# Top-k attention and a tanh-shrink FFN on one core: batch 0's key and query rows in 256-byte runs turned by TensorE, weight exponents by one ScalarE operation

## The chip, the core and the metric

The kernel runs on one core of a Trainium2 chip. The metric is the device time of one execution in microseconds (us), lower is better. All inputs and outputs lie in the chip's memory; transfers go through the core's 16 DMA engines. Five engines run their own instruction queues in order and wait for each other on semaphores: TensorE (PE in the profile, with its weight loads as PEld), VectorE (DVE), ScalarE (ACT), GpSimd (POOL) and SyncE (SP), which only issues DMAs here.

## What is computed

The reference does attention with 8 batches, 8 heads, 576 tokens and a head size of 64. Of each row of scores only the 32 largest stay. The result, 4608 rows of 512, goes through a two-layer network with a tanh shrink.

```python
scores = scale * np.matmul(q, k.transpose(0, 1, 3, 2))
kth = np.partition(scores, -top_k, axis=-1)[..., -top_k:-top_k + 1]   # top_k = 32
scores = np.where(scores >= kth, scores, -1e9)
attn = np.exp(scores - np.max(scores, axis=-1, keepdims=True))
attn = attn / (np.sum(attn, axis=-1, keepdims=True) + 1e-09)
x = np.matmul(attn, v)            # then (B, H, S, D) -> (B*S, H*D) = (4608, 512)
h = x @ w_in                      # (512, 2048)
out = (h - np.tanh(h)) @ w_out    # (2048, 512)
```

q, k and v arrive as 32-bit floats. The weights w_in and w_out arrive as 64-bit floats, and the kernel turns them into 32-bit floats itself.

## The kernel before

**Steps.** The attention is cut into steps. A step takes two heads (a head pair `hp`, 0 to 3) of one batch and 128 query rows (`qt`), or the 64 rows that are left over of two pairs. The order is written out by hand (`tc.manual_schedule()`): the main loop in `run` goes over `n` and issues, for each `n`, work of several steps at once: the top-32 search of step n (`search`), the mask of step n-1 (`mask`), the turning of the probabilities of step n-2 (`turn_pe` while batch 0 lasts, `turn_z` after it), the scores of step n+1 (`scores`), the exponentials of step n-1 (`expo`), and pieces of the network (`ffn_h`, `ffn_o`), which `deal` hands out at a rate worked out from the steps alone. The program is therefore the same list per engine whatever the times are; only the waits move.

**What a step asks of each engine.** VectorE does the search: two passes that split the scores into larger and smaller halves (L268, L269), a check (L271), and then four rounds of "eight largest" (L276) with three "replace these eight" (L279). ScalarE copies the scores out of PSUM (L246), makes the mask (L308) and the exponentials (L331). GpSimd makes the thresholds (L295), subtracts the mask (L311, two instructions of 1.4 us back to back) and notes suspicious rows (L315). TensorE makes the scores (L238), turns the probabilities in batch 0 (L425, with ScalarE copying the result out of PSUM in L428), multiplies by v (L453) and does the network (L504, L525).

**Batch 0.** Its first four steps, n = 0 to 3, are the four head pairs with query rows 0 to 127. The keys and queries of all four pairs are loaded ahead of the loop's first steps by `load_rows`, in the order pair 0, weight piece 0, pair 1, weight piece 1, and so on. Pair 0 goes to a load buffer; pairs 1 to 3 go to `early`, slices of `w_in[2]` and `w_in[3]`, whose place is free until those weights are converted. One `load_rows` makes four DMAs. Each has 32 partitions with 18 runs of 32 floats (128 bytes) in each, so that a plain 32 by 32 block transpose on VectorE (`turn_rows`, L223) gives the keys or queries with the head dimension on the partitions. Pair hp is turned during step hp-1, after the first round of the search (`at_round[(n - 1, 0)]`), keys and queries one after the other. `scores` of step hp wait for both. The PSUM pool `zt_ps`, two buffers, serves `turn_pe` and `values`.

**Weights.** `convert` handles a piece of 128 by 512 weights. Two DMAs of 512 KB bring it (L148 as it is, L149 shifted by three bytes). Then:

- VectorE takes the 11 exponent bits (L158), ScalarE clamps and rescales them in two operations (L159, L162), VectorE cuts the mantissa (L164), ScalarE scales it (L167);
- VectorE joins sign and exponent (L170), where L162's result lies in PSUM for the 16 pieces of w_in (`e`) and in SBUF for the 16 pieces of w_out (`f`, in place);
- GpSimd multiplies the two (L173).

Pieces 0 and 1 belong to step 0, pieces 2 and 3 to step 1, three pieces to each of steps 2 to 9, four to step 10. Within a step the parts are spread over the rounds of the search, the first after round 0, behind the turning of keys and queries. A piece's buffer is loaded again when L173 has been issued; seven buffers exist at the start.

Of the kernel before, what the change touches and what calls it, by code (L numbers as in the profile page):

```python
# [8 lines left out]
AF = mybir.ActivationFunctionType  # L9
ALU = mybir.AluOpType  # L10
FP32 = mybir.dt.float32
I32 = mybir.dt.int32
# [7 lines left out]
J = 4  # L20
# [29 lines left out]
def kernel(  # L50
# [9 lines left out]
    nc = tc.nc  # L60
    P = nc.NUM_PARTITIONS
    B, H, S, D = q.shape
    DM, DFF = moe_w_in.shape
    NHP = H // 2
    JP = J * P
    R = S - JP
# [10 lines left out]
    scale = 1.0 / float(D) ** 0.5  # L77
# [5 lines left out]
    def pool(name, bufs, **kw):  # L83
        return ctx.enter_context(tc.tile_pool(name=name, bufs=bufs, **kw))

    consts = pool("consts", 1)
# [12 lines left out]
    zt_ps = pool("zt_ps", 2, space=PS)  # L99
    h_ps = pool("h_ps", 2, space=PS)  # L100

    ident = consts.tile([P, P], FP32, name="ident")
# [3 lines left out]
    w_in = [consts.tile([P, CD, DFF // WJ], FP32, name=f"w_in{j}") for j in range(WJ)]  # L106
# [8 lines left out]
    zx1 = consts.tile([P, 4 * S], FP32, name="zx")[:]  # L115
    et2 = [consts.tile([P, 4 * S], FP32, name="et")[:], later[:, 0 : 4 * S]]
    et_rem = later[:, 4 * S : 6 * S]
    e1151 = consts.tile([P, 1], FP32, name="e1151")
    nc.gpsimd.memset(e1151[:], 1151.0 * 2.0**23)
    e255 = consts.tile([P, 1], FP32, name="e255")  # L120
    nc.gpsimd.memset(e255[:], 255.0 * 2.0**23)

    def flat(x):
        return x.rearrange("p n w -> p (n w)")
# [13 lines left out]
    def convert(piece, slot):  # L138


        j, i = piece // CD, piece % CD
        if j < WJ:
            src, dst = moe_w_in[i * P : (i + 1) * P, j * NW : (j + 1) * NW], w_in[j][:, i, :]
        else:
            r0 = ((j - WJ) * FJ + i) * P
            src, dst = moe_w_out[r0 : r0 + P, :], w_out[j - WJ][:, i, :]
        raw, shifted, _ = slot
        nc.sync.dma_start(flat(raw), src.bitcast(U32))  # L148
        nc.sync.dma_start(  # L149
            flat(shifted).bitcast(U8)[:, 0 : 8 * NW - 4], src.bitcast(U8)[:, 3 : 8 * NW - 1]  # L150
        )
        yield
        hi = raw[:, :, 1]
        f = thpool.tile([P, NW], FP32, tag="th", name="f")
        fu = f[:].bitcast(U32)


        nc.vector.tensor_scalar(fu, hi, 20, 0x7FF, ALU.logical_shift_right, ALU.bitwise_and)  # L158
        nc.scalar.activation(f[:], fu, AF.Relu, bias=e1151[:], scale=-(2.0**23))  # L159

        e = h_ps.tile([P, NW], FP32, tag="h", name="e")[:] if j < WJ else f[:]
        nc.scalar.activation(e.bitcast(I32), f[:], AF.Relu, bias=e255[:], scale=-1.0)  # L162

        nc.vector.tensor_scalar(  # L164
            dst.bitcast(U32), shifted[:, :, 0], 0x0FFFFFFF, None, ALU.bitwise_and
        )
        nc.scalar.activation(dst, dst.bitcast(U32), AF.Copy, bias=1.0, scale=2.0**-28)  # L167
        yield

        nc.vector.scalar_tensor_tensor(  # L170
            out=fu, in0=hi, scalar=0x80000000, in1=e.bitcast(U32), op0=ALU.bitwise_and, op1=ALU.bitwise_or
        )
        nc.gpsimd.tensor_tensor(dst, dst, f[:], ALU.mult)  # L173
        yield
# [3 lines left out]
    raw, kT, qT, vb, vr = {}, {}, {}, {}, {}  # L178
# [5 lines left out]
    def half(t):  # L184
        return slice(t * D, (t + 1) * D)


    early = [flat(w_in[j][:])[:, i * S : (i + 1) * S] for j in (2, 3) for i in range(3)]

    def load_rows(name, b, hp, exact):  # L190

        if b == 0 and hp and not exact:
            x = early[2 * hp - 2 + (name == "q")]
        else:
            x = ldpool.tile([P, S], FP32, tag=f"{name}in", name=f"{name}in")[:]
        raw[name, b, hp] = x
        src = {"k": k, "q": q}[name]
        for a in range(NG):
            h, d = 2 * hp + a // 2, a % 2 * G
            queue = nc.scalar if a and (name, b, hp, exact) == ("q", 0, 0, False) else nc.sync  # L200
            queue.dma_start(  # L201
                x[a * G : (a + 1) * G, :].rearrange("i (n d) -> i n d", d=G),
                src[b, h, :, d : d + G].rearrange("(n i) d -> i n d", i=G),
            )

    def load_v(b, hp):
# [4 lines left out]
        for t in range(2):  # L211
# [4 lines left out]
            o = 0 if t else JP  # L216
            nc.sync.dma_start(y[half(t), t, :], v[b, h, o : o + R, :])

    def turn_rows(name, b, hp):

        d = kqpool.tile([P, S], FP32, tag=f"{name}T", name=f"{name}T")
        {"k": kT, "q": qT}[name][b, hp] = d
        nc.vector.transpose(d[:], raw.pop((name, b, hp)))  # L223

# [183 lines left out]
    def turn_pe(n):  # L410

        g, z = steps[n], st.pop(n)["z"]
        if g.rem:
            et = et_rem
        elif g.i:
            et = ets.pop(n - 1)
        else:
            et = et2[0]
        ets[n] = et
        et = tiles(et, g.nq)[:, :, :, g.i, :].rearrange("p a k j -> p k a j")  # L420
        for k0 in range(0, KC, J):
            kn = min(J, KC - k0)
            zt = zt_ps.tile([P, 512], FP32, tag="zt", name="zt")
            for k in range(kn):
                nc.tensor.transpose(  # L425
                    zt[:, k * P : (k + 1) * P], z[:, (k0 + k) * P : (k0 + k + 1) * P], ident[:]
                )
            nc.scalar.copy(  # L428
                et[:, k0 : k0 + kn],
                zt[:, 0 : kn * P].rearrange("p (k a j) -> p k a j", a=NG, j=G),  # L430
            )
            if k0:
                yield
# [119 lines left out]
    def plan():  # L553
        steps.clear(), done.clear()

        def block(b, qt):
            return [(slice(0, P), out[b * S + qt * P : b * S + (qt + 1) * P, :])]

        rest = None
        for b in range(B):  # L560
            if b % 2 == 0:
                rest = Unit(
                    [[(half(i), out[(b + i) * S + JP : (b + i + 1) * S, :]) for i in range(2)]], "xTr"
                )

            parts = [(0, 1), (2, 3)]
            if b == 0:
                parts[0:1] = [(0,), (1,)]
            for a, qts in enumerate(parts):
                unit = Unit([block(b, qt) for qt in qts], "xT")  # L570
                pe = b == 0
                for hp in range(NHP):
                    for i, qt in enumerate(qts):
                        steps.append(Step(b, hp, qt, unit, 0, i, len(qts), pe))
                    if hp == NHP - 1:
                        done[len(steps) - 1] = unit
                    if hp % 2 and a == (0 if b == B - 1 else len(parts) - 1):
                        steps.append(Step(b, hp - 1, J, rest, b % 2 * R, pe=pe))
                        if hp == NHP - 1 and b % 2:
                            done[len(steps) - 1] = rest  # L580
        for g, after in zip(steps, steps[1:]):
            if after.pe and not after.rem and not g.pe:
                g.lag = 3
# [3 lines left out]

    def run(exact):
        plan()
        NS = len(steps)  # L590
        todo, at_round, turned = {}, {}, {}

# [5 lines left out]
        for i, (b, hp) in enumerate(pairs):  # L598
            n = next(n for n, g in enumerate(steps) if (g.b, g.hp) == (b, hp))
            for x, name in enumerate("kq"):  # L600
                m = max(n - 5 + x, turned.get(name, -4))
                if b == 0 and not exact:
                    m = -4
                at(m, lambda x=(name, b, hp, exact): load_rows(*x))
                if x and i < NHP and not exact:
                    at(-4, lambda: load_piece())
                turn = lambda x=(name, b, hp): turn_rows(*x)
                if 0 < i < NHP:
                    at_round.setdefault((n - 1, 0), []).append(turn)
                    turned[name] = n - 1  # L610
                else:
                    at(n - 3 + x, turn)
                    turned[name] = n - 3 + x
            at(n + 1 if b else n - 1, lambda b=b, hp=hp: load_v(b, hp))
# [41 lines left out]
        def here(i):  # L656
            return 0 <= n + i < NS

# [25 lines left out]
        def rate():  # L684
# [3 lines left out]
            coming = sorted((t, u.n // 8) for u, t in ready.items() if t > n)  # L688
            for t, k in coming + [(NS + LAG, 0)]:
                r = have / max(t - n, 1)  # L690
# [18 lines left out]

        for n in range(-4, NS + LAG):  # L710
            pe = here(-2) and steps[n - 2].pe
            for m in (n - LAG, n - LAG + 1, n - LAG + 2):
                if 0 <= m < NS and steps[m].last and steps[m].lag == n - m:
                    values(m)
            share, usable = rate(), converted[0]
            if pe:
                w = turn_pe(n - 2)
# [74 lines left out]
```

## Time and profile before

| | |
|---|---|
| time, median of 3 (lowest to highest) | 1534.32 us (1533.35 to 1534.38) |
| span of the profiled execution | 1533.0 us |
| busy: TensorE, VectorE, ScalarE, GpSimd | 1432.2, 1349.9, 1021.6, 871.3 us |
| chain that ended last, by engine | TensorE 75%, VectorE 13%, ScalarE 5%, SyncE 2%, DMA 2% |
| VectorE's start of the search (L268) in steps 0 to 11 | 10.31, 22.41, 35.58, 49.07, 61.77, 73.92, 86.19, 99.16, 115.04, 128.80, 146.21, 163.18 us |
| L223, keys and queries of pairs 1 to 3 | 3 x 768 ns and 3 x 736 ns |
| L159 | 32 x 711 ns |
| L162 | 16 x 692 ns into PSUM, 16 x 722 ns into SBUF |
| L428, ScalarE copy out of PSUM | 589 ns for 512 columns, 267 ns for 128 |

Busy times are sums over a whole run and hide that the kernel has stages. Two tools of the profile show them: the span cut into slices with the busy share of each engine, and the timeline, in which every row is one instruction (or several of a kind, xN) with its start, its duration, and in brackets how long its engine sat idle before it and what it waited for. A duration can itself hold a wait that no semaphore shows.

### The profile page before, as it was taken

What the parts mean: (1) busy time and instruction counts of PE and PEld (TensorE: products, weight loads), DVE (VectorE), ACT (ScalarE), POOL (GpSimd) and SP (SyncE); (2) the same over time, 40 slices, a digit from 0 to 9 for tenths busy, and PEclk for the clock granted to TensorE, in tenths of its full rate; (3) what the DMA queues carried; (4) which work ended last, traced back from release to release, by engine and by line L of the source; (5) the groups of instructions that cost most, each with busy time, mean ns of one, the idle gap of its engine ahead of it and who ended that gap; (6) DMA issues with size and microseconds to landing.
All of it is one profiled execution on the core that took longest, in us unless ns stands there. A gap on an engine that the chain in (4) does not pass through costs nothing.

```text
span 1533.0 us, 24064 instructions
## 1 busy us (share of the span) xinstructions
PE 1432.2 (93%) x7302; PEld 901.9 (59%) x7302; DVE 1349.9 (88%) x3884; ACT 1021.6 (67%) x1833; POOL 871.3 (57%) x1371
## 2 busy tenths in 40 slices
PE   2567898999999999999999999999999999999997
PEld 1355566456465675656575665656565665656673
DVE  7998999999999999999999999999999999997100
ACT  4887777667676676767676676767676676767320
POOL 3777676656474564647474574647475574746210
PEclk9887999999999999999999999999999999999999
DMA  9944113556755666556655565556655666543400
GB/s 256 358 169 161 50 24 95 148 142 163 168 140 176 144 151 156 140 157 153 171 136 157 144 157 165 138 144 157 174 140 148 148 155 164 140 140 91 137 8 16
DMA packets 255467, 221.61 MB, mean 145 GB/s; under 512 B 197728, under 2 KB 204896, under 8 KB 248160
## 3 DMA queue, kind: packets, MB, share of 16 engines
q1 hardware_dynamic: 253552, 219.75, 53.4%
q8 instruction: 60, 0.98, 0.3%
q14 instruction: 79, 0.65, 0.2%
q10 hardware_dynamic: 1776, 0.22, 0.1%
HBM read 136.17 MB, written 83.76 MB: 143 GB/s over the span
## 4 chain that ended last, share of the span: by engine, by line
PE 75%; DVE 13%; ACT 5%; SPq 2%; DMA 2%; POOL 1%; issue 1%; DVEq 0%; ACTq 0%; POOLq 0%
PE ops L525 29%; PE hps L504 28%; PE av L453 9%; PE scps L238 8%; DVE m L276 3%; DVE ab L279 3%; DVE zx L388 2%; SPq L201 1%; DVE ab L269 1%; DVE ab L271 1%; DVE ab L268 1%; DMA zx<-in_moe_w_in_dram 1%; PE zt L425 1%; ACT z L308 1%; ACT sc L246 1%
## 5 line engine op out<-in xcount | busy, mean ns | idle before, releaser
L525 PE MATMUL ops<-w_out,g 128*128 128x512 f32 x1152 | 525.6, 603 | 0.0
L311 POOL TENSOR_TENSOR z<-sc,z 128x576 f32<-128x576 f32 x288 | 401.0, 1415 | 209.0 <-ACT z L308 209.0
L504 PE MATMUL hps<-xT,w_in 128*128 128x256 f32 (+1 forms) x2176 | 475.1, 374 | 0.5 <-ACT g L517 0.4
L276 DVE MAX8 m<-ab 128x8 f32<-128x288 f32 (+1 forms) x1152 | 468.4, 450 | 0.0
L504 PEld LDWEIGHTS hps<-xT,w_in 128*128 128x128 f32 x2176 | 391.6, 193 | 82.5 <-issue 32.3
L279 DVE MATCH_REPLACE8 ab<-m,ab 128x288 f32<-128x288 f32 x864 | 377.2, 446 | 0.0
L525 PEld LDWEIGHTS ops<-w_out,g 128*128 128x128 f32 x1152 | 211.3, 191 | 256.8 <-issue 240.6
L518 POOL TENSOR_TENSOR g<-g,th 128x512 f32<-128x512 f32 x144 | 182.8, 1274 | 159.3 <-ACT g L517 154.5
L308 ACT ACTIVATE z<-sc,tb 128x576 f32<-128x576 f32 x288 | 207.6, 769 | 89.7 <-POOL tb L295 78.2
L238 PE MATMUL scps<-kT,qT 64*128 64x288 f32 (+1 forms) x1280 | 188.2, 445 | 42.3 <-DVE qT L223 27.1
L331 ACT ACTIVATE z<-z,nb 128x576 f32<-128x576 f32 x288 | 221.2, 771 | 2.5 <-POOL z L311 2.4
L388 DVE STREAM_TRANSPOSE zx<-z 128x1152 f32<-128x1152 f32 x126 | 172.6, 1370 | 42.8 <-ACT z L357 42.5
L357 ACT ACTIVATE z<-z,rd 128x576 f32<-128x576 f32 x252 | 180.3, 763 | 44.3 <-DVE rd L350 44.3
L238 PEld LDWEIGHTS scps<-kT,qT 64*128 64x128 f32 (+1 forms) x1280 | 102.3, 184 | 130.4 <-issue 42.4
L246 ACT COPY sc<-scps 128x1152 f32<-128x1152 f32 x144 | 159.2, 1105 | 11.3 <-PE scps L238 10.2
L341 POOL TENSOR_SCALAR rd<-den 128x2 f32<-128x2 f32 x144 | 33.5, 233 | 198.6 <-ACT z L331 197.6
L516 ACT ACTIVATE th<-hps 128x512 f32<-128x512 f32 x144 | 84.8, 589 | 89.9 <-PE hps L504 87.5
L268 DVE TENSOR_TENSOR ab<-scps,sc 128x576 f32<-128x576 f32 x144 | 105.7, 734 | 13.9 <-ACT sc L246 6.5
L271 DVE MAX8 ab<-ab 128x8 f32<-128x288 f32 x288 | 116.2, 445 | 0.0
L269 DVE TENSOR_TENSOR ab<-scps,sc 128x576 f32<-128x576 f32 x144 | 107.4, 746 | 0.0
L453 PE MATMUL av<-et,vb 128*64 128x256 f32 (+1 forms) x640 | 77.2, 373 | 30.4 <-ACT et L428 30.4
L535 ACT COPY ot<-ops 128x512 f32<-128x512 f32 x36 | 21.0, 584 | 114.3 <-PE ops L525 114.3
(70 smaller groups left out, 1157.5 us busy)
## 6 DMA issues: line engine op xcount, KB each, us to landing
there<-zx SPq DMA_DIRECT2D x56, 1152.0 KB, 4.2
spare<-there SPq DMA_DIRECT2D x112, 288.0 KB, 5.3
et<-there SPq DMA_DIRECT2D x112, 288.0 KB, 5.1
kin<-in_k_dram SPq DMA_DIRECT2D x116, 72.0 KB, 2.4
vb<-in_v_dram SPq DMA_DIRECT2D x64, 128.0 KB, 5.7
out_dram<-ot SPq DMA_DIRECT2D x32, 256.0 KB, 2.3
qin<-in_q_dram SPq DMA_DIRECT2D x113, 72.0 KB, 3.1
there<-zx SPq DMA_DIRECT2D x14, 576.0 KB, 4.8
```

The lines of the kernel that those rows point to most:

```text
L238: nc.tensor.matmul(ps[rows, t, s, 0:S2], qT[g.b, g.hp + i][half(t), qs], kT[g.b, g.hp + i][half(t), ks], start=True, stop=True,)
L276: nc.vector.max(m[:, t, m8], last[t] if i == rounds - 1 else cur[t])
L279: nc.vector.match_replace(nxt[t], m[:, t, m8], cur[t], NEG)
L308: nc.scalar.activation(zv[:, t, :], scf[:, t, :], AF.Relu, bias=tb[:, t : t + 1], scale=-BIG)
L311: nc.gpsimd.tensor_tensor(zv[:, t, :], scf[:, t, :], zv[:, t, :], ALU.subtract)
L331: nc.scalar.activation(x["zv"][:, t, :], x["zv"][:, t, :], AF.Exp, bias=x["nb"][:, t : t + 1], scale=scale, accum_out=den[:, t : t + 1],)
L357: nc.scalar.activation(x, x, AF.Copy, scale=rds[n][:, g.i, t : t + 1])
L388: nc.vector.transpose(tiles(zx, g.nq)[:, :, :, g.i, :].rearrange("p c k j -> p k c j"), z[:].rearrange("p (k c j) -> p k c j", c=NG, j=G),)
L453: nc.tensor.matmul(av[half(t), 0, cols], vb[g.b, hp][:, t, c, :] if c < J else vr[g.b, hp][:, t, :], es[:, :, (J + 1) * t + c if c < J els ...
L504: nc.tensor.matmul(cur[u][:, s : s + w], w_in[j][:, c, fo : fo + P], u.xT[:, c, 0:w], start=(c == 0), stop=(c == CD - 1),)
L518: nc.gpsimd.tensor_tensor(g, g, th[:], ALU.subtract)
L525: nc.tensor.matmul(cur[u][:], u.g[o // 1024][:, o % 1024 // 512, o % 512 : o % 512 + P], w_out[f // FJ][:, f % FJ, :], start=(f == 0), sto ...
```

## The change

Two edits. The first makes the loads of the keys and queries of batch 0's pairs 1 to 3 in runs of 256 bytes: tokens lie on the partitions, and for each head one DMA brings 512 tokens (128 partitions, 4 runs each) and one brings the last 64. Such rows can't be turned by VectorE's 32 by 32 transpose; TensorE turns them, four 128 by 128 transposes and one of 64 rows for each of keys and queries, and ScalarE copies the two PSUM tiles out. A row is then 640 floats wide, so the `early` slices grow. The second edit makes the exponent of a weight with one ScalarE operation in place of two. Its aim is less work on ScalarE, the first one's is fewer small transfers at the start and less work on VectorE.

```diff
-    e1151 = consts.tile([P, 1], FP32, name="e1151")
-    nc.gpsimd.memset(e1151[:], 1151.0 * 2.0**23)
-    e255 = consts.tile([P, 1], FP32, name="e255")
-    nc.gpsimd.memset(e255[:], 255.0 * 2.0**23)
+    e896 = consts.tile([P, 1], FP32, name="e896")
+    nc.gpsimd.memset(e896[:], -896.0 * 2.0**23)
...
         nc.vector.tensor_scalar(fu, hi, 20, 0x7FF, ALU.logical_shift_right, ALU.bitwise_and)
-        nc.scalar.activation(f[:], fu, AF.Relu, bias=e1151[:], scale=-(2.0**23))
         e = h_ps.tile([P, NW], FP32, tag="h", name="e")[:] if j < WJ else f[:]
-        nc.scalar.activation(e.bitcast(I32), f[:], AF.Relu, bias=e255[:], scale=-1.0)
+        nc.scalar.activation(e.bitcast(I32), fu, AF.Relu, bias=e896[:], scale=2.0**23)
...
-    early = [flat(w_in[j][:])[:, i * S : (i + 1) * S] for j in (2, 3) for i in range(3)]
+    early = [flat(w_in[j][:])[:, 5 * i * P : 5 * (i + 1) * P] for j in (2, 3) for i in range(3)]
...
+        if b == 0 and hp and not exact:
+            xv = x.rearrange("p (c t d) -> p t c d", t=2, d=D)
+            for t in range(2):
+                h = 2 * hp + t
+                nc.sync.dma_start(
+                    xv[:, t, 0:J, :], src[b, h, 0:JP, :].rearrange("(c p) d -> p c d", p=P)
+                )
+                nc.sync.dma_start(xv[0:R, t, J, :], src[b, h, JP:S, :])
+            return
...
-        nc.vector.transpose(d[:], raw.pop((name, b, hp)))
+        x = raw.pop((name, b, hp))
+        if not (b == 0 and hp and turned_pe[0]):
+            nc.vector.transpose(d[:], x)
+            return
+        for c0, c1, w in ((0, J, P), (J, J + 1, R)):
+            zt = zt_ps.tile([P, 512], FP32, tag="zt", name="zt")
+            for c in range(c0, c1):
+                o = (c - c0) * P
+                nc.tensor.transpose(zt[:, o : o + w], x[0:w, c * P : (c + 1) * P], ident[0:w, 0:w])
+            w = (c1 - c0 - 1) * P + w
+            nc.scalar.copy(d[:, c0 * P : c0 * P + w], zt[:, 0:w])
```

More of the change, by code (lines that the diff above doesn't have):

```diff
@@ L217, in load_v @@
             nc.sync.dma_start(y[half(t), t, :], v[b, h, o : o + R, :])
+    turned_pe = [True]
     def turn_rows(name, b, hp):
@@ L589, in run @@
         plan()
+        turned_pe[0] = not exact
         NS = len(steps)
```

## The prediction, made before the changed kernel was built

> **What bounds the kernel now.** I read the slices of the span first, then busy time by stretches, then the waits and the timeline of the start, since the change touches only steps 0 to 10.
>
> ```profile
> PE   2567898999999999999999999999999999999997
> DVE  7998999999999999999999999999999999997100
> ACT  4887777667676676767676676767676676767320
> ```
>
> A slice is 38.3 us. TensorE is not full in the first six slices and full from there to the end; VectorE is nearly full from the second slice.
>
> ```profile
> 0.00:38.00 38.00, 8.84 (x32) 5.23 (x32) 27.40 (x72) 16.55 (x25) 11.68 (x27) 1.00 1.04 256
> 38.00:76.00 38.00, 20.75 (x109) 14.45 (x110) 36.54 (x105) 32.13 (x58) 28.05 (x37) 0.84 0.99 358
> 76.00:115.00 39.00, 25.80 (x192) 21.41 (x190) 35.20 (x99) 33.14 (x60) 28.86 (x37) 0.85 0.48 171
> 115.00:153.00 38.00, 27.70 (x153) 20.40 (x153) 30.71 (x83) 29.88 (x57) 28.58 (x38) 0.73 0.45 162
> 268.00:400.00 132.00, 123.17 (x584) 70.38 (x583) 132.00 (x387) 92.50 (x165) 79.17 (x131) 0.99 0.58 150
> 600.00:800.00 200.00, 200.00 (x976) 126.78 (x974) 193.43 (x557) 140.86 (x254) 120.21 (x192) 1.00 0.58 150
> ```
>
> Columns: stretch, length, busy time of TensorE, its weight loads, VectorE, ScalarE, GpSimd, then clock, DMA share and GB/s. Up to 38 us the DMAs are full (1.04) at only 256 GB/s: small packets. To 76 us VectorE is the fullest engine, 36.54 of 38. From 76 to 153 us no engine is full, so the steps hang on a loop through several. At 268 to 400 us VectorE is busy 132.00 of 132, later TensorE 200.00 of 200. Work after step 10 is unchanged and in the same order, and its limits are those two engines. So **what the start saves moves the end one for one**, and nothing else can.
>
> Who waits for whom on VectorE, first up to 60 us, then 60 to 160 us (total, times, longest):
>
> ```profile
> DVE w_in L164 <- DMA w_out<-in_moe_w_in_dram: 3.5, 3, 1.3
> DVE f L158 <- DMA w_out<-in_moe_w_in_dram: 1.7, 2, 1.3
> DVE f L170 <- ACT f L162: 10.9, 4, 4.6
> ```
>
> In steps 0 and 1 VectorE waits for weight pieces, behind the small packets on the rings; in steps 7 to 10 it waits for the exponent, the operation that the second edit shortens.
>
> **What the Trainium skill says.** Three places. "SBUF — State Buffer", section "Who interferes with whom": VectorE in a two-port mode, or with two SBUF inputs, and a GpSimd instruction exclude each other, and the second to issue blocks until the first is done. The trace agrees:
>
> ```profile
> 25.08 2.76 POOL L311 TENSOR_TENSOR z<-sc,z 128x576 f32<-128x576 f32 x2 [0.41 <-ACT z L308]
> 26.03 0.77 DVE L223 STREAM_TRANSPOSE kT<-w_in 128x576 f32<-128x576 f32 x1
> 26.72 0.73 DVE L223 STREAM_TRANSPOSE qT<-w_in 128x576 f32<-128x576 f32 x1
> 27.39 0.74 DVE L158 TENSOR_SCALAR f<-w_out 128x512 uint32<-128x512 uint32 x1
> ```
>
> L158 takes 0.41 us where GpSimd is quiet; here 0.74, ending at 28.13, 0.29 after L311's end at 27.84. L223 isn't held up. L170 with `f` in SBUF (w_out) takes 0.68 free and 1.35 against L311; with `e` in PSUM it is never held.
>
> "DMA: Bandwidth & Descriptors", section "Why small descriptors are slow (HBM only)": a fixed cost of about 3 cycles per packet, 11 cycles for 256 bytes; by the same rule 7 for 128 bytes, an estimate, so 256 bytes cost 1.57 times as much. The packet records up to 60 us give 15.5 ns per packet of 128 bytes and 18.0 of 256 (1.16 times); over the whole run 13.6 and 21.4 (1.57 times, in agreement).
>
> "TensorE: Matmul & The Clock Gate", section "Part 4: PE-mode transpose": the transpose ends in PSUM and needs a copy; some 275 ns each in a kernel. Row L425 shows eight in 1.97 us at 34.72, 246 ns each, and I use that.
>
> **The change part by part.**
>
> *Loads.* 24 DMAs of 576 packets, 13,824 packets of 128 bytes, become 6,912 of 256. On 16 engines: 13,824 x 15.5 / 16 = 13.4 us become 7.8 us (18.0 ns), 9.2 (21.4 ns) or 10.5 (1.57 x 15.5). Saved: 5.6, 4.2 or 2.9 us. I take 4.2. SyncE's issues number 24 both times; the v loads of the same new shape cost it 0.4 to 0.65 us each, and the present ones about 0.8[...]; nothing is lost there. Piece 1 lies behind two of the six loads (1.4 us earlier), piece 3 behind all.
>
> *Turning.* Off VectorE: in each of steps 0 to 2, 0.77 + 0.73 less overlap, 1.36 us (26.03 to 27.39). On TensorE: 5 transposes per turn, 1.2 us, while it is idle for 29 of the first 38 us. On ScalarE: 0.59 + about 0.22 per turn (L428, from 512 columns and from 128), 1.6 us per step. Behind these copies on ScalarE stand the step's conversions, and the queries' transposes wait for the keys' copies since `zt_ps` has two buffers: about 4 us until both are there. In steps 1 and 2 they follow L308, after which ScalarE idles 2.50 us before L159 now; L159's removal gives back 0.71 per piece. The scores that wait for the turn are needed only at the next L268, 8 us later. **Cost on the path: nothing.**
>
> *Exponent.* 32 x 711 ns, 22.7 us off ScalarE. The one operation that stays is taken at L162's 0.69 and 0.72; nothing shows it with integers on both sides, so 0.6 to 0.75. Its worth depends on what the step hangs on.
>
> *Step 0 and 1.* Step 0: VectorE comes to piece 1 1.36 us sooner but piece 1 only 1.4 to 1.9 sooner: gain 1.4 to 1.9, say 1.6. Step 1: without L223, L158 arrives at 26.03 of the old clock, inside the first of the two L311 (25.08 to 26.45). If it gets the port between the two, it ends at 26.8 in place of 28.13: gain 1.3. Then the DMA waits of piece 3 (0.41 + 0.86) fall away if the piece comes 4.2 us sooner. 1.6 + 1.3 + 1.3 = 4.2; the DMA allows 2.9 to 5.6. **4.0 taken.**
>
> *Step 2.* L158 at 40.55 takes 1.18 us, ending 0.29 after L311 at 41.45. Without L223 it arrives at 39.20, in the first L311, and goes at 40.07: **gain 1.3**, or 0 if the port is not given up.
>
> *Steps 3 to 5.* Here ScalarE looks critical, but the lock decides:
>
> ```profile
> 66.58 2.89 POOL L311 TENSOR_TENSOR z<-sc,z 128x576 f32<-128x576 f32 x2 [1.37 <-ACT z L308]
> 68.53 0.69 DVE L170 SCALAR_TENSOR_TENSOR f<-w_out,e 128x512 uint32<-128x512 uint32 x1
> 69.13 0.61 DVE L158 TENSOR_SCALAR f<-spare 128x512 uint32<-128x512 uint32 x1
> ```
>
> L158 of the third piece waits for L311's end (69.47) and ends 0.28 later. Getting there 0.4 to 0.6 us sooner only lengthens its wait. L311 hangs on L308, that on TensorE's turn (L425, L428), that on GpSimd's L369 behind L173, that on VectorE's L170: a loop of 12.2 us without L159 in it. **Gain 0.**
>
> *Steps 6 to 10.* The same loop, but now the first L170 has two SBUF inputs:
>
> ```profile
> 107.00 2.79 POOL L311 TENSOR_TENSOR z<-sc,z 128x576 f32<-128x576 f32 x2 [2.45 <-ACT z L308]
> 107.47 0.72 ACT L159 ACTIVATE f<-f,e 128x512 f32<-128x512 uint32 x1
> 108.22 0.72 ACT L162 ACTIVATE f<-f,e 128x512 int32<-128x512 f32 x1
> 108.97 1.35 DVE L170 SCALAR_TENSOR_TENSOR f<-spare,f 128x512 uint32<-128x512 uint32 x1 [3.07 <-ACT f L162]
> ```
>
> L170 misses the gap between the two L311 (108.37) and waits for the second (109.79). Without L159 the exponent is there at 108.2, 0.1 to 0.2 before the gap; the same in steps 8, 9, 10. If L170 gets in, it ends 1.35 sooner, of which about 0.8 reaches the next step, since GpSimd's own queue (L311, L315, two L173) then sets the third L170. If not, 0.1. Steps 7 to 10: 3.2 or 0.4. **2.5 taken**, because VectorE did get in between L311 and L315, as at 28.13.
>
> Sum: 4.0 + 1.3 + 0 + 2.5 = 7.8 us. 1534.3 - 7.8 = 1526.5.
>
> **Rivals.**
>
> *The lock is never given up between two L311.* Then removing L223 buys only waiting; the DMA waits go (1.3 + 1.3) and 0.5 elsewhere: 3.1 us, 1531.2. For it: the two L311 start back to back. Against: the L315 case.
>
> *ScalarE is the bound from step 3.* Then every wait for it goes: 10.9 (above) plus 1.2 for L246 and 0.6 for the PSUM exponent, 12.7, plus the 5.3 of steps 0 to 2: 18 us, 1516.3. For it: the chain of waits names L159, L162, L167 and L246 in a row from 76 to 160 us. Against: the lock and the loop, which it doesn't show.
>
> *The turn adds waits.* ScalarE and TensorE need about 4 us for what took VectorE 1.5; if the 2.6 us show up in three steps, 7.8 us stand against the 4.0 saved by the loads: 1538.1, slower. For it: conversions queue behind the copies. Against: the idle 2.50 us before L159.
>
> **How the numbers follow.** Forecast 0.50, lock 0.21, ScalarE 0.20, turn 0.09. The bounds of the forecast itself are 1522 to 1531. Faster by over 0.2% (under 1531.2): 0.50 + half of the lock case 0.10 + 0.20 = 0.80. Within 0.2%: the rest of the lock case and a small turn cost, 0.13. Slower 0.07. Range 1515.5 to 1533: it takes in the ScalarE case and the lock case and leaves out the turn case and the tails.
>
> **What would show it.** L164 of step 0 should wait for a DMA under 1.3 us and those of step 1 not at all; L268 of step 3 should start some 5 us sooner (44 us); steps 3 to 5 should still last 12.2 us each with L158 of the third piece ending 0.3 after L311; steps 7 to 10 should show L170 of the first w_out piece between the two L311. From step 11 on, spacings should be unchanged. The prediction is wrong if steps 4 to 6 become much shorter than 12 us, if L238 waits for L428-like copies into the next L268, or if time gained by 163 us is given back before 400 us.

## The result and the profile after

The changed kernel takes **1527.41 us** (median of 6 runs, 1526.02 to 1529.87) against 1533.62 us of the kernel before on the same chip (6 runs, 1532.89 to 1534.38): ratio 0.9962, 95% interval 0.9949 to 0.9974. The profiled span went from 1533.0 to 1526.4 us.

The diff moves line numbers. After the change L286 starts the search (before: L268), L329 is the mask subtraction on GpSimd (L311), L155, L160 and L166 are VectorE's three parts of a weight piece (L158, L164, L170), L158 is the exponent (L159 and L162), L169 GpSimd's product (L173). L239 and L241 are the new transposes and copies; L233 is what is left of the transpose on VectorE.

The slices of the span, answering to those of before:

```profile
PE   4567898999999999999999999999999999999997
DVE  7998999999999999999999999999999999997100
ACT  4776777767676676767676676767676676767320
```

TensorE's first digit rose from 2 to 4 (the turns), ScalarE's second to fourth fell by one each, its eighth rose by one. The same stretches as before (columns: stretch, length, busy TensorE, weight loads, VectorE, ScalarE, GpSimd, clock, DMA share, GB/s):

```profile
0.00:38.00 38.00, 16.47 (x61) 10.25 (x61) 28.39 (x74) 18.06 (x32) 13.81 (x29) 1.00 1.01 282
38.00:76.00 38.00, 22.08 (x123) 15.39 (x123) 38.00 (x107) 27.28 (x53) 29.46 (x38) 0.75 1.02 359
76.00:115.00 39.00, 26.26 (x188) 21.53 (x187) 36.83 (x96) 27.25 (x53) 31.79 (x38) 0.76 0.47 168
115.00:153.00 38.00, 29.30 (x156) 19.59 (x155) 33.43 (x91) 26.27 (x48) 31.31 (x38) 0.82 0.47 165
268.00:400.00 132.00, 122.72 (x568) 69.02 (x566) 132.00 (x382) 93.08 (x166) 77.59 (x129) 0.99 0.65 158
```

The DMAs are as full up to 38 us but bring 282 GB/s in place of 256. ScalarE lost 4.85 of 32.13 us (38 to 76 us) and 5.89 of 33.14 (76 to 115 us). VectorE gained busy time in every stretch up to 153 us: it is at 38.00 of 38 where it was at 36.54. Work after 268 us looks as before. VectorE's waits as the view lists them, to 60 us (three lines) and from 60 to 160 us (one; each with total, times, longest):

```profile
DVE kT L233 <- DMA kin<-in_k_dram: 6.7, 1, 6.7
DVE ab L286 <- ACT sc L264: 1.7, 1, 1.7
DVE w_in L160 <- DMA w_out<-in_moe_w_in_dram: 1.2, 2, 1.0
DVE f L166 <- ACT f L158: 6.7, 4, 2.8
```

Waits for weight pieces fell from 5.2 to 1.2 us, and those for the exponent in SBUF from 10.9 to 6.7. Against that, the first wait, for the keys of pair 0, grew from 5.3 to 6.7 us, and a wait of 1.7 us for the first scores is new. In all VectorE waits 16.3 us here and 23.4 before: 7.1 us less, and the kernel is 6.2 us faster. Where each part was gained is read from the starts of the search, taken from the timelines; `e5` is the same changed kernel run on another chip, and its profile is of the slowest of its five runs:

| steps | forecast gain | changed kernel | `e5` |
|---|---|---|---|
| 0 and 1 | 4.0 us | 2.64 | 2.76 |
| 2 | 1.3 | 0.16 | 0.14 |
| 3 to 5 | 0 | 0.48 | 0.49 |
| 6 to 10 | 2.5 | 2.44 | 0.58 |
| 11 and 12 | 0 | 0.97 | 0.30 |
| up to step 13 | 7.8 | 6.69 | 4.27 |

The search of step 0 itself starts later than before, at 11.66 us in place of 10.31, because pair 0's keys are turned at 6.68 us in place of 5.33. This goes with the second edit: in all ten profiles with it the turn starts between 6.49 and 6.87 us, in the four without it between 5.15 and 5.42. No run shows why. The gain of steps 0 and 1 is what is left after this loss.

From step 13 on, the changed kernel is ahead by a nearly constant 6.69 us: 6.66 to 6.83 in every step to 140.

### The profile page after: what moved, and what is told of

Same layout as the page of the kernel before. It is cut to its first block, busy times and chain, and to the rows that moved or that the text cites. A ratio compares the mean times of both kernels' runs of the same rounds, so it can differ in the third digit from the quotient of the medians.

```text
span 1526.4 us, 24131 instructions
## 1 busy us (share of the span) xinstructions
PE 1438.1 (94%) x7332; PEld 904.4 (59%) x7332; DVE 1352.0 (89%) x3878; ACT 1002.8 (66%) x1813; POOL 875.8 (57%) x1370
## 4 chain that ended last, share of the span: by engine, by line
PE 73%; DVE 20%; ACT 3%; POOL 1%; issue 1%; DMA 1%; DVEq 0%; ACTq 0%; SPq 0%; POOLq 0%
PE ops L543 28%; PE hps L522 28%; PE av L471 9%; PE scps L256 8%; DVE m L294 5%; DVE ab L297 5%; DVE zx L406 2%; DVE ab L289 1%; DVE ab L287 1%; DVE ab L286 1%; DVE f L155 1%; DVE f L166 1%; ACT z L349 1%; ACT z L326 1%; DVE w_in L160 0%
## 5 line engine op out<-in xcount | busy, mean ns | idle before, releaser
L329 POOL TENSOR_TENSOR z<-sc,z 128x576 f32<-128x576 f32 x288 | 403.2, 1422 | 203.9 <-ACT z L326 203.6
L326 ACT ACTIVATE z<-sc,tb 128x576 f32<-128x576 f32 x288 | 207.6, 769 | 88.4 <-POOL tb L313 76.9
L286 DVE TENSOR_TENSOR ab<-scps,sc 128x576 f32<-128x576 f32 x144 | 105.0, 729 | 13.0 <-ACT sc L264 6.9
L313 POOL TENSOR_SCALAR tb<-m 128x1 f32<-128x1 f32 x288 | 88.4, 316 | 7.1 <-DVE m L294 0.2
```

The lines of the kernel that those rows point to most:

```text
L326: nc.scalar.activation(zv[:, t, :], scf[:, t, :], AF.Relu, bias=tb[:, t : t + 1], scale=-BIG)
L329: nc.gpsimd.tensor_tensor(zv[:, t, :], scf[:, t, :], zv[:, t, :], ALU.subtract)
```

## The experiments

All ratios are to the kernel before, run beside each kernel on the same chip.

**e1, the second edit alone.** The loads and L223 stay as before.

```diff
-        nc.scalar.activation(f[:], fu, AF.Relu, bias=e1151[:], scale=-(2.0**23))
-        nc.scalar.activation(e.bitcast(I32), f[:], AF.Relu, bias=e255[:], scale=-1.0)
+        nc.scalar.activation(e.bitcast(I32), fu, AF.Relu, bias=e896[:], scale=2.0**23)
```

> The second edit alone: loads of 128-byte runs and VectorE's turn as before, exponents by one ScalarE operation. Theory A (loads matter to step 3, exponent from there on): L268 of step 3 within 0.4 us of before (49.07), then about 3.5 us gained in steps 3 to 12: 1530.1 us. Theory B (ScalarE bounds the start, the loads did nothing): nearly the whole gain, 1527.5 to 1528. Theory C (the exponent is hidden, the loads are all of it): 1533.5.

Measured: 1531.94 us, ratio 0.9984 (0.9977 to 0.999), about two thirds of theory A's gain. Step 3 starts 0.06 us sooner than before, step 11 1.64. So this edit alone gains nothing at the start: what step 0 loses by its later begin, the shorter waits for weight pieces give back.

**e2, the first edit alone.** The exponent keeps its two operations.

> The first edit alone: loads of 256-byte runs and the turn on TensorE, exponents by two ScalarE operations. Theory A: L268 of step 3 about 2.8 us sooner than before, step lengths from there on as before (12.7, 12.2, 12.3, 13.0, 15.9): 1530.8 us. Theory B: the turn's copies queue ahead of longer conversions, no gain or a loss: 1533.5 to 1535. Theory C: 1527.5.

Measured: 1531.19 us, 0.9979 (0.9972 to 0.9986). The two edits add up: 0.16% and 0.21%, and 0.38% together. But step 3 starts only 1.71 us sooner, where both edits together have 2.80, and step 11 starts 3.08 us sooner, 1.61 of it from step 6 to step 10 where this edit changes nothing. Something else varies in those steps. The start varies as well: step 0 lasted 11.63 us here and 10.58 in e12 below, whose instructions are the same up to there.

**e5, the changed kernel again**, on another chip, as the base for e6 to e8.

> The changed kernel once more, unedited, beside the three below. Expected 1528.2 us on a chip where the kernel before takes 1534.4 (ratio 0.996). Step lengths 7, 9 and 12 should vary with where the throttle takes TensorE's clock away, the others repeat within 0.1 us.

Measured: 1528.17 us against 1534.81, 0.9956 (0.9943 to 0.9969). What varies shows when step 7 is cut out of the changed kernel's trace and out of e5's (columns as above, one line from each, in this order; the third line is from e4 below, which changes only steps 1 and 2):

```profile
96.19:111.76 15.57, 11.10 (x86) 9.85 (x86) 13.40 (x36) 9.92 (x21) 11.69 (x14) 0.87 0.56 205
96.09:112.78 16.69, 12.47 (x86) 11.04 (x86) 13.40 (x35) 10.02 (x21) 11.70 (x14) 0.80 0.56 193
95.48:109.61 14.13, 9.66 (x86) 8.41 (x86) 13.39 (x35) 9.91 (x21) 11.69 (x14) 0.99 0.64 225
```

The same list of instructions, the same VectorE time, but a clock of 0.87, 0.80 or 0.99 and 11.10, 12.47 or 9.66 us of TensorE: the step lasts 15.57, 16.69 or 14.13 us, each time 4.2 to 4.5 us more than TensorE's busy time. Step 9 behaves alike (16.21 at 0.89, 16.86 at 0.84). So step 7 of a single profile can be off by over 2 us and steps 9 and 12 by about 1; the medians are the better measure.

**e3, runs of 128 bytes again, turned by TensorE.** Each load of 512 tokens is cut in two along the head dimension; so are those of the last 64 tokens (not shown), with both heads in one DMA.

```diff
+                for d in (0, G):
+                    nc.sync.dma_start(
+                        xv[:, t, 0:J, d : d + G],
+                        src[b, h, 0:JP, d : d + G].rearrange("(c p) d -> p c d", p=P),
+                    )
...
```

> The changed kernel with the same rows and the same turn on TensorE, but its loads cut into runs of 128 bytes again (13,824 packets). If the packets made the gain of steps 0 and 1, the waits of L160 and L155 for weight pieces come back (about 1.3 us in step 0 and 1.3 in step 1) and the time is about 1529.8 us. If VectorE's relief from six transposes made it, it stays at 1527.4 us.

Measured: 1537.19 us, 1.0028 (1.0017 to 1.0039), slower even than the kernel before. But it wasn't only the packets. SyncE's queue for pair 1, and the share of the 16 DMA engines used up to 45 us (the time of all packets over the time of 16 engines, which can pass 100%):

```profile
4.89 2.36 SPq L200 DMA_DIRECT2D w_in<-in_k_dram  x4
7.29 2.57 SPq L205 DMA_DIRECT2D w_in<-in_k_dram  x2
9.91 2.25 SPq L200 DMA_DIRECT2D w_in<-in_q_dram  x4
12.20 1.26 SPq L205 DMA_DIRECT2D w_in<-in_q_dram  x2
```

```profile
q1 hardware_dynamic: 19287, 9.18, 78.9%
```

Twelve issues take 8.6 us (4.89 to 13.46), where the changed kernel's eight take 5.4 and the eight of before 6.7. The engines are 78.9% busy, against 97.9% in the changed kernel and 100.8% before. A weight piece behind the issues comes late, and VectorE waits for it 5.5 us in one go. The cut doubled the packets and raised the issues from 24 to 36, so it can't tell the two apart by itself; e6 and e7 do.

**e6 and e7, packet size at equal issues.** The two heads of a pair are taken as one list of 1152 rows, loaded by two DMAs. In e6 each DMA takes part of the rows in whole 256-byte runs (6,912 packets); in e7 each takes all rows and half the head dimension, 128-byte runs (13,824 packets). Both turn with 11 TensorE products per name (that part is not shown). The comments say which line belongs to which run.

```diff
+            rows = src[b, 2 * hp : 2 * hp + 2].rearrange("t s d -> (t s) d")
+            rows = rows.rearrange("(c p) d -> p c d", p=P)
+            for cs, ds in ((slice(0, 5), slice(0, D)), (slice(5, 9), slice(0, D))):   # e6
+            for cs, ds in ((slice(0, 9), slice(0, G)), (slice(0, 9), slice(G, D))):   # e7
+                nc.sync.dma_start(xv[:, cs, ds], rows[:, cs, ds])
```

> The changed kernel with keys and queries of a pair loaded as 1152 rows in two DMAs (not four), still in 6,912 packets of 256 bytes; TensorE turns 128 by 64 blocks. If SyncE's issues bound the loads, weight pieces land sooner than in the changed kernel, but VectorE waits there for only 0.23 us in step 0 and nothing in step 1: same time as the changed kernel within 1 us, either way. It is the partner of the next one.

> As the partner, two DMAs for a pair, but each in runs of 128 bytes (13,824 packets). Theory packets: the DMA engines spend 13.4 in place of 8 to 9 us on them, pieces 1 and 3 come 1.4 and 4 us later, VectorE waits 1.3 us in step 0 and about 1 in step 1: 2 to 3 us over the partner. Theory issues (what bound the loads is how many DMAs SyncE has to issue and wait for): within 0.7 us of the partner.

Measured: 1531.13 us, 0.9977 (0.9969 to 0.9986), and 1532.54 us, 0.9987 (0.9981 to 0.9994). Step 3 starts 2.91 us sooner than before in e6, as in e5, and 0.68 sooner in e7. VectorE's waits for weight pieces up to 60 us, e6's line first, then e7's two:

```profile
DVE w_in L160 <- DMA w_out<-in_moe_w_in_dram: 1.0, 1, 1.0
```

```profile
DVE w_in L160 <- DMA w_out<-in_moe_w_in_dram: 3.0, 3, 1.2
DVE f L155 <- DMA w_out<-in_moe_w_in_dram: 0.3, 1, 0.3
```

So of the 2.9 us by step 3, packet size gives 2.2, and what takes work off VectorE, together with the fewer issues, some 0.7. These are single profiles, but e1, with small packets and no TensorE turn, stands with e7 (0.06 us sooner), and e5 with e6. The medians are less clear: they lie 1.4 us apart, between the 2 to 3 us and the 0.7 that the two theories expected, and their intervals overlap; by step 13 e7 is even ahead (4.53 us sooner than before, e6 4.22), since its steps 7, 9 and 12 came out shorter. e7 also sheds light on e3: with as many packets in 12 issues the engines are 106.2% busy up to 45 us, against e3's 78.9% with 36, which points to the issues. e6's median stays 3 us behind e5's, although at step 13 the two are level (4.22 and 4.27). Its profile is longer by 1.6 us behind the last output copy, 9.3 us against 7.7 (e7: 8.8); why is not explained.

**e8, every turn done twice.** The second turn writes the same values again.

```diff
-        for c0, c1, w in ((0, J, P), (J, J + 1, R)):
+        for c0, c1, w in 2 * ((0, J, P), (J, J + 1, R)):
```

> The changed kernel doing each turn of keys and queries twice (the same transposes and copies again into the same place: 30 more transposes, 12 more copies of 0.2 to 0.6 us on ScalarE, about 1.6 us more per step on it). Theory hidden: step lengths 0 to 3 unchanged within 0.3 us, time of the changed kernel. Theory exposed: conversions come later, L166 waits for the exponent in steps 1 and 2, 1 to 3 us slower.

Measured: 1532.82 us, 0.9989 (0.9981 to 0.9997), 4.6 us above e5. Step 3 starts 5.1 us later than in the changed kernel, for VectorE now waits for the exponent behind the copies:

```profile
DVE f L166 <- ACT e L158: 4.9, 2, 4.7
```

One turn is hidden: up to 60 us the changed kernel's VectorE has no wait for an exponent. A second one is not. In step 2, which lasts 17.20 us in place of 13.34, the last of the doubled copies are these, and the exponent stands right behind them:

```profile
44.16 0.70 ACT L241 COPY qT<-zt 128x512 f32<-128x512 f32 x2 [1.14 <-PE zt L239]
44.74 0.71 ACT L158 ACTIVATE e<-f,e 128x512 int32<-128x512 uint32 x1
```

The copies start at 38.69, 40.52, 42.31 and 44.16 us: ScalarE copies for 0.70 us and then idles until TensorE has turned the next. So a turn holds up ScalarE's queue for some 1.8 us, not for the 0.8 of its copies. With one turn of keys and queries L158 follows 2.3 us behind the mask (L326), within the 2.50 us that ScalarE idled before; with two it follows 6.0 us behind.

**e4, the conversion of steps 1 and 2 kept out of GpSimd's way.** The parts that stood behind round 0 of the search go behind round 1, and in step 2 those behind rounds 1 and 2 go a round later too; the rest of the changed kernel stays.

```diff
+            late = {1: (1, 1, 2, 3), 2: (1, 1, 2, 2, 3, 3)}
             for i, x in enumerate(seq):
-                at_round.setdefault((m, 3 * i // max(len(seq) - 1, 1)), []).append(
-                    lambda x=x: part(*x)
-                )
+                r = 3 * i // max(len(seq) - 1, 1)
+                if m in late:
+                    r = late[m][i]
+                at_round.setdefault((m, r), []).append(lambda x=x: part(*x))
```

> The changed kernel with the first conversion parts of steps 1 and 2 moved from round 0 to round 1 of the search, so that L155 and L160 come after both subtractions on GpSimd (L329) and not between them. If the port took back what the turn gave, L160 falls from 1.62 to about 0.42 us in steps 1 and 2, step 1 lasts about 10.4 us in place of 11.57 and step 2 about 12.3 in place of 13.34: 1525.2 us. If the weight pieces bound these steps, VectorE waits for a DMA at L155 of piece 3 and the time stays at 1527.4 us.

The reason for it is in step 1 of the changed kernel (start, duration, then the idle time in brackets):

```profile
24.04 2.94 POOL L329 TENSOR_TENSOR z<-sc,z 128x576 f32<-128x576 f32 x2 [0.41 <-ACT z L326]
24.99 0.74 DVE L155 TENSOR_SCALAR f<-w_out 128x512 uint32<-128x512 uint32 x1
25.65 1.62 DVE L160 TENSOR_SCALAR w_in<-w_out 128x512 uint32<-128x512 uint32 x1
```

The row of L329 holds both subtractions; the first ends at 25.45. L155 gets in between the two, as forecast, and ends at 25.73. L160 right behind it, 0.41 us when free, is then held through the second L329, which ends at 26.98, and ends itself at 27.27, 0.29 later. In e4:

```profile
26.91 0.52 DVE L155 TENSOR_SCALAR f<-w_out 128x512 uint32<-128x512 uint32 x1
27.35 0.41 DVE L160 TENSOR_SCALAR w_in<-w_out 128x512 uint32<-128x512 uint32 x1
27.68 0.44 DVE L155 TENSOR_SCALAR f<-w_out 128x512 uint32<-128x512 uint32 x1
28.93 0.43 DVE L160 TENSOR_SCALAR w_in<-w_out 128x512 uint32<-128x512 uint32 x1 [0.81 <-DMA w_out<-in_moe_w_in_dram]
```

L160 takes 0.41; the hold is gone, and most of it returns as a 0.81 us wait for the next piece, so that step 1 is only 0.49 us shorter (11.08 in place of 11.57). Step 2 lasts 12.05 us in place of 13.34, and step 3 starts 4.23 us sooner than before, against 2.80; e9 and e10, with the same order in these two steps, have 4.38 and 4.08. The median doesn't show it: 1527.63 us, 0.9962 (0.9949 to 0.9976). Its interval spans 4 us, and step 3's further 1.4 us can't be seen in that.

**e9 and e10, the same for steps 3 to 9.** In e9 the parts that stood behind round 1 go behind round 2, and those behind round 2 behind round 3, so that none meets L329. e10 puts L155 and L160 of all three pieces of a step behind round 0, ahead of L329, and the three L166 behind rounds 1, 2 and 3. Both keep e4's table for steps 1 and 2. The lines shown are e10's.

```diff
+            front = m > 2 and len(mine) == 3
+            if front:
+                seq.sort()
...
+                elif front and x[0] == 1:
+                    r = 0
+                elif front:
+                    r = min(1 + x[1] - mine[0], 3)
```

> The changed kernel with conversion parts moved out of the time of the two subtractions in all steps: steps 1 and 2 from round 0 to 1, steps 3 to 9 from round 1 to round 2 (and the last two parts to round 3). Theory port: the blocked L155 and L160 (1.2 to 1.6 us each) fall to 0.42; steps 1, 2 as in the run with those two alone (11.1, 12.1), steps 3 to 6 about 11.7 in place of 12.2 to 13.3: 4 to 5 us less than the changed kernel, ratio 0.993. Theory loop: with the parts later, GpSimd's multiplications L169 come later, the loop over L387 and TensorE's turn gets longer, nothing gained: ratio 0.996.

> The changed kernel with the first parts (L155, L160) of all three pieces of a step in round 0, ahead of the two subtractions, in steps 3 to 9, and L166 of the three pieces in rounds 1, 2 and 3; steps 1 and 2 moved to round 1 as before. Theory port: no two-port instruction meets the subtractions in steps 3 to 5, which then last about 11.7 us (in place of 12.2); in steps 6 to 9 only one L166 waits, about 0.5 us less each: ratio 0.993. Theory loop: steps 3 to 5 keep 12.2 us, since L169 of the third piece still ends them: ratio 0.996.

Measured: e9 1523.87 us, 0.9926 (0.9913 to 0.9938); e10 **1522.64 us, 0.9923 (0.991 to 0.9936)**, which beats the kernel before and the changed one. In e9 steps 4 and 5 last 11.58 us each, in place of 12.20 and 12.21. Step 4 of e10:

```profile
60.71 0.43 DVE L155 TENSOR_SCALAR f<-w_out 128x512 uint32<-128x512 uint32 x1
...
62.07 0.41 DVE L155 TENSOR_SCALAR f<-spare 128x512 uint32<-128x512 uint32 x1
62.40 0.41 DVE L160 TENSOR_SCALAR w_in<-spare 128x512 uint32<-128x512 uint32 x1
62.71 2.78 POOL L329 TENSOR_TENSOR z<-sc,z 128x576 f32<-128x576 f32 x2 [0.53 <-ACT z L326]
```

Six conversion parts run at their free 0.41 to 0.43 us, ending (62.81) as L329 begins. Steps 4 and 5 last 11.39 and 11.38 us; step 3, at 12.09 in place of 12.22, hardly gained.

**e11 and e12, which part of e10 is the order's.** e11 is the kernel before with e10's order, without both edits; e12 has the first edit and e10's order.

> The kernel before with neither edit of the change, but the conversion parts moved as in the run with all first parts in round 0 (steps 1, 2 to round 1). Theory port (the port hid part of what the change is worth): the order alone brings 2 to 4 us (ratio 0.998), DMA waits of steps 0 and 1 remain, so the change on top of this order is worth more (0.9923 against 0.998, 0.57%) than on the old order (0.4%). Theory that order and change are independent: ratio 0.9963.

> The first edit alone with that new order, exponents by two ScalarE operations. If the exponent edit is worth more once VectorE's port is clear, this is 3 to 4 us behind the run with both edits (ratio 0.995) and VectorE waits for the exponent in steps 3 to 6 (L169 <- ScalarE). If it is worth as little as on the old order (2.4 us) or less: 0.994 or lower.

Measured: e11 1531.89 us, 0.9989 (0.9982 to 0.9995); e12 1529.11 us, 0.9963 (0.9949 to 0.9977). The order alone brings little, 0.11%. Had order and change been independent, e11 would have come to 0.9963, which its interval excludes: the two together are worth more than their sum. Between e12 and e10 only the exponent differs, and it is worth 0.40% there (0.9963 to 0.9923, worked out from the two ratios; about 6 us), where it was 0.16% in the old order. The two intervals allow 0.13 to 0.67% for it, so the size is rough, but the steps show the same. Step 4 of e12 and of e10 (columns as above), and the start of e12's step 5:

```profile
57.57:69.64 12.07, 6.73 (x38) 4.66 (x38) 11.46 (x34) 11.14 (x22) 9.73 (x14) 0.64 0.94 352
57.08:68.48 11.40, 7.28 (x43) 5.08 (x44) 11.40 (x36) 9.44 (x19) 9.96 (x14) 0.65 1.05 386
69.64 0.76 DVE L289 TENSOR_TENSOR ab<-scps,sc 128x576 f32<-128x576 f32 x1 [0.61 <-ACT sc L267]
```

With two operations ScalarE is busy 11.14 of 12.07 us, its copy of the scores (L267) comes late, and VectorE waits 0.61 us for it. With one, ScalarE has 9.44 us of work, that wait is gone, and VectorE is busy throughout.

## Why the prediction was right, and where its steps were not

The forecast of 1526.5 us is 0.9 us from the measured 1527.4. The gain is further off, 6.2 us in place of 7.8, because the kernel before came out 0.7 us lower than the 1534.3 that the forecast started from. And there is luck in the sum: 2.5 us too little in steps 0 to 2 stand against 0.48 and 0.97 us that were not forecast, and a good part of steps 6 to 12 varies from run to run.

**What the start saves moves the end one for one: right.** The lead of 6.69 us at step 13 is there at step 140.

**Loads, 4.2 us: right.** The packet records up to 60 us give 20.4 ns per packet of 256 bytes, so 6,912 x 20.4 / 16 = 8.8 us in place of 13.4: 4.6 us saved. That is 1.3 times the time per packet; the estimate of 1.57 that I worked out from the Trainium skill ("DMA: Bandwidth & Descriptors", "Why small descriptors are slow (HBM only)") would have been 24.3 ns and fits the whole run but not this stage. e6 against e7 shows that the packets, more than the relief of VectorE, carry the start.

**Steps 0 to 2, 5.3 us forecast, 2.8 measured: the failed step.** It was the term "If it gets the port between the two", 1.3 us in step 1 and 1.3 in step 2. (The port is the access to the on-chip memory SBUF for which VectorE and GpSimd exclude each other, as in the first of the prediction's three places.) The instruction did get in, and so the lock rival, in which the port is never given up, is wrong as a mechanism. But the term stopped at that one instruction. The port then goes back to GpSimd, and L160 loses what L155 gained. Step 2 repeats it. So the lock rival's amount for these steps, the 1.3 + 1.3 us of DMA waits, was nearer than mine. e4 shows this by taking the conversion out of the way: step 2 shortens by 1.29 us, the size of the term, and in step 1 the 0.49 us gained and the 0.81 us that became a wait for a piece make 1.30. Another 0.6 us of the miss lie in step 0: it became 2.40 us shorter, but began 1.35 us later, which the forecast had not, and 1.04 is left of the 1.6.

**The turn costs nothing: right, with a thin margin.** Against the rival in which it adds waits stand the 2.6 us lead at step 2 and VectorE's list of waits, which has none for a turn or an exponent up to 60 us; for it, that a second turn cost 4.6 us. The 0.59 + 0.22 us per copy pair was right (0.57 to 0.59 and 0.21 to 0.22); the transposes of a turn took 1.38 to 1.41 us in place of 1.2.

**Steps 3 to 5, nothing: right within 0.48 us, by the lock named.** Step 4 after the change:

```profile
63.88 2.77 POOL L329 TENSOR_TENSOR z<-sc,z 128x576 f32<-128x576 f32 x2
65.10 0.67 DVE L166 SCALAR_TENSOR_TENSOR f<-w_out,e 128x512 uint32<-128x512 uint32 x1
65.69 1.24 DVE L155 TENSOR_SCALAR f<-spare 128x512 uint32<-128x512 uint32 x1
```

The third piece's L155 arrives sooner and waits longer, 1.24 us where it took 0.61, and ends 0.28 us after L329 (66.65 to 66.93). The hold, 1.24 less the free 0.41, is 0.83 us, and 0.81 is what e10, which has no hold there, takes off this step. The loop through four engines that the prediction added was not tested apart from it; VectorE, with the held time counted, is busy through the whole step (12.19 of 12.19 us). The ScalarE rival (18 us) is refuted for this order: steps 3 to 5 kept their 12.2 us.

**Steps 6 to 10, 2.5 us: the size came out by luck.** Step 7 after the change:

```profile
103.86 3.23 POOL L329 TENSOR_TENSOR z<-sc,z 128x576 f32<-128x576 f32 x2 [2.30 <-ACT z L326]
104.34 0.72 ACT L158 ACTIVATE f<-f,e 128x512 int32<-128x512 uint32 x1
105.08 0.74 DVE L166 SCALAR_TENSOR_TENSOR f<-spare,f 128x512 uint32<-128x512 uint32 x1 [2.17 <-ACT f L158]
105.74 1.63 DVE L155 TENSOR_SCALAR f<-w_out 128x512 uint32<-128x512 uint32 x1
```

L166 gets in between the two L329 in 0.74 us where it took 1.35, as forecast. But L155 behind it is held for 1.63, and the pair of L329 takes 3.23 in place of 2.79. Cut out by steps, VectorE's column tells the rest; steps 7 and 9 of the kernel before:

```profile
99.16:115.04 15.88, 11.23 (x86) 10.05 (x86) 12.81 (x35) 11.90 (x23) 11.65 (x14) 0.89 0.55 200
128.80:146.21 17.41, 11.95 (x62) 8.69 (x62) 12.81 (x35) 13.08 (x26) 12.12 (x15) 0.79 0.48 174
```

and step 9 of the changed kernel, whose step 7 was shown with e5:

```profile
125.36:141.57 16.21, 11.13 (x62) 7.64 (x62) 13.40 (x35) 10.69 (x21) 12.16 (x15) 0.89 0.50 185
```

The same list of VectorE instructions costs 13.40 us in both steps in place of 12.81. In step 7 the difference is 1.22 us more in the held L155 (1.63 against 0.41) less 0.61 saved in L166: what ScalarE gave back, and 0.6 us more, turned into waiting for the port, counted as busy. What was left is small in the steps that hardly vary: step 6 is 0.3 us longer, step 8 0.2 shorter, step 10 1.1 shorter (15.9 us with the edit, 17.0 without). The rest of the 2.44 us lies in steps 7 and 9; e5 has 0.58 us in all, and e2, without the edit, 1.61, and e5's step 7 ties it to the TensorE clock. An estimate for step 7 takes TensorE's busy time off its length: 4.65 us are left in the kernel before and 4.59 in e2, 4.20 to 4.49 in the eight runs with the edit and the old order there, so that the edit earns 0.1 to 0.45 us of the 0.8 forecast for a step. Which share of a median it earns in all these steps stays open; for the whole kernel it is e1's 0.16%.

**Steps 11 and 12, nothing: 0.97 us measured.** Nearly all of it is step 12, 9.46 us in place of 10.43, which took 10.14 in e5 with the same program. So most of it is variation between runs and not the edits' work.

**Where the rest of the gain was.** e10 against e12 shows it: once the conversion's parts don't meet L329, the exponent edit is worth 0.40% by the medians, and about 0.7 us in each of steps 4 and 5, where it had gained 0.3 us at most (e2 against the changed kernel: 12.51 and 12.16 against 12.20 and 12.21). The ScalarE rival had seen this much rightly, that ScalarE's work was worth more than I gave it, but it needed the port cleared first.

## What to carry to other kernels

Where VectorE and GpSimd exclude each other, follow the port past the one instruction that gets in: ask what VectorE issues next, since that one may be held for the whole of GpSimd's next instruction. A gain that ends in a longer duration, and not in a wait, is a sign of it, and moving the work to a stretch where the other engine is idle can be worth more than shortening it. When the cost of small transfers is tested, keep the number of DMA issues equal; and check whether steps that the edit doesn't touch move as well, before a profile's difference is put down to the edit.

## What the hardware showed that was not expected

- In steps 1, 2 and 7 a held VectorE instruction took its turn when the running GpSimd instruction ended, and then the waiting GpSimd one went ahead of VectorE's next (in step 1 0.74 us, then 1.62). The Trainium skill ("SBUF — State Buffer", "Who interferes with whom") tells of the blocking; the alternation is what these traces add.
- The exponent with integers on both sides takes 0.688 us into PSUM and 0.715 into SBUF, as the second of the two removed operations did (0.692 and 0.722).
- The same number of small packets at the start, 13,824, left the DMA engines 78.9% busy up to 45 us in 36 issues (e3), 100.8% in 24 (the kernel before) and 106.2% in 12 (e7).
- The same instructions of step 7 lasted 14.13, 15.57 or 16.69 us, with the TensorE clock at 0.99, 0.87 or 0.80.
